# GroupNorm on one core: GpSimd scales 13 channels of a tile instead of 8 and ScalarE three instead of two, so VectorE's share goes from 22 to 16

## The chip, the cores and the metric

The kernel runs on one core of a Trainium2 chip. The metric is device time in microseconds (us). Time before the change: 635.31 us, the median of three runs (635.22 to 635.34). In the profiles PE is TensorE, DVE is VectorE, ACT is ScalarE, POOL is GpSimd and SP is SyncE.

## The reference

`x` is 128 x 1024 x 32 x 16 in bf16, in 32 groups of 32 channels.

```python
def reference(x, g, b):
    G = 32
    ...
    xr = x.reshape(B, G, C // G, H, W)
    mu = xr.mean(axis=(2, 3, 4), keepdims=True)
    var = ((xr - mu) ** 2).mean(axis=(2, 3, 4), keepdims=True)
    xn = (xr - mu) / jnp.sqrt(var + 1e-5)
    xn = xn.reshape(B, C, H, W)
    return xn * g[None, :, None, None] + b[None, :, None, None]
```

## The kernel before

One tile is 128 partitions (4 samples x 32 groups) by 32 channels of 512 numbers: 4 MB. There are 32 tiles. For each tile TensorE sums the channels with 32 matmuls against the unit matrix, VectorE reduces that to the mean, ScalarE sums the squares in two halves, and then the 32 channels are scaled in place, one instruction a channel, because each channel has its own factor and offset. SyncE issues one 4 MB load and one 4 MB store a tile (the first and the last tile's loads and the last two tiles' stores go in four parts). Six tiles fit into memory.

```python
ACT_SHARE = 2
LAST_SHARE = 2      # channels of a tile that ScalarE scales
POOL_SHARE = 8      # channels of a tile that GpSimd scales
...
    def scale_on(key, i, k):
        st = state[i]
        span = st["xt"][:, k * HW : (k + 1) * HW]
        scl = st["scl"][:, k : k + 1]
        bia = st["bia"][:, k : k + 1]
        if key == "act":
            inst = nc.scalar.activation(
                out=span, in_=span, func=ACT.Identity, bias=bia, scale=scl
            )
        else:
            eng = nc.vector if key == "dve" else nc.gpsimd
            inst = eng.tensor_scalar(
                out=span, in0=span, scalar1=scl, scalar2=bia,
                op0=ALU.mult, op1=ALU.add,
            )
        chain(key, inst)
...
    def A(i):
        if not in_parts(i):                 # all tiles but the last two
            for n in range(POOL_SHARE):
                scale_on("pool", i, KC - LAST_SHARE - POOL_SHARE + n)
            for k in range(KC - LAST_SHARE - POOL_SHARE):
                scale_on("dve", i, k)
            ...
    def finish(i):                          # called between the two halves of the next tile's squares
        ...
        for k in range(KC - LAST_SHARE, KC):
            scale_on("act", i, k)
        S(i, 0, NQ)                         # the store
        state.pop(i)
        j = i + AHEAD
        if UPFRONT <= j < NT:
            L(j)                            # the next load, into the buffer of tile i - 1
```

Of the kernel before, what the change touches and what calls it, by code (L numbers as in the profile page):

```python
# [21 lines left out]
QUARTERS = 4  # L22
STORE_IN_PARTS = 2
ACT_SHARE = 2
LAST_SHARE = 2
POOL_SHARE = 8


@with_exitstack
def kernel(  # L30
# [326 lines left out]
# [12 lines that stand above are left out]
                out=span,  # L369
                in0=span,  # L370
                scalar1=scl,
                scalar2=bia,
                op0=ALU.mult,
                op1=ALU.add,
            )
        chain(key, inst)
# [10 lines left out]
    def in_parts(i):  # L387
        return i >= NT - STORE_IN_PARTS

    def A(i):  # L390

        if not in_parts(i):
# [4 lines that stand above are left out]
# [11 lines left out]
    def finish(i):  # L408
        if i < 0 or in_parts(i):
            return  # L410
        for k in range(KC - LAST_SHARE, KC):
            scale_on("act", i, k)
# [47 lines left out]
```

## Time and profile before

| what | before |
|---|---|
| median, us | 635.31 |
| span of the profiled run, us | 633.4 |
| DMA, 130 to 530 us | 431 GB/s, share 1.00 |
| busy: ScalarE, VectorE, PE, GpSimd | 82%, 58%, 46%, 36% |

The costliest groups before (line, engine, operation, names, shapes, count | busy us, mean ns | idle before them and what ended it):

```profile
L244 ACT ACTIVATE ja<-xt,negmean 128x8192 fp8e5<-128x8192 bf16 x60 | 426.7, 7112 | 74.7 <-DVE jd L189 74.7
...
L368 DVE TENSOR_SCALAR xt<-xt,scl,bia 128x512 bf16<-128x512 bf16 x716 | 341.3, 552 | 39.8 <-POOL bia L353 39.8
...
L368 POOL TENSOR_SCALAR xt<-xt,scl,bia 128x512 bf16<-128x512 bf16 x240 | 190.5, 805 | 3.3
...
L363 ACT ACTIVATE xt<-xt,bia,scl 128x512 bf16<-128x512 bf16 x68 | 50.8, 798 | 0.8 <-DVE bia L324 0.8
```

One tile before, from the timeline (start us, length us, engine, what): the scaling on VectorE and GpSimd, the next tile's sum, and SyncE's next load and store.

```profile
320.03 10.76 DVE L368 TENSOR_SCALAR xt<-xt,scl,bia 128x512 bf16<-128x512 bf16 x22 [1.28 <-POOL bia L353]
320.10 6.35 POOL L368 TENSOR_SCALAR xt<-xt,scl,bia 128x512 bf16<-128x512 bf16 x8
...
338.29 0.69 DVE L189 TENSOR_SCALAR_CACHE_REDUCE jd<-pa 128x512 bf16<-128x512 f32 x1 [7.50 <-PE pa L166]
...
338.99 0.34 SPq L101 DMA_DIRECT2D xt<-in_x_dram  x1
...
339.44 0.36 SPq L381 DMA_DIRECT2D out_dram<-xt  x1
```

The scaling is over at 330.8 us, VectorE then idles 7.5 us, and the tile's store leaves at 339.4 us, behind a load. The DMA queue's own list of waits says for what that load had stood (us in total, times, longest us):

```profile
SPq L101 <- DMA out_dram<-xt: 451.3, 26, 19.5
```

The load waits for an earlier store to land, because it goes into that store's buffer. So engine time is spare and DMA time is not. Three stretches before, from the table of stretches (busy us of PE, PEld, DVE, ACT, POOL, then clock, DMA share, GB/s):

```profile
130.00:530.00 400.00, 189.55 (x658) 73.60 (x659) 241.63 (x522) 333.14 (x145) 156.82 (x250) 0.72 1.00 431
...
625.00:630.00 5.00, 0.00 (x0) 0.00 (x0) 0.00 (x0) 0.00 (x0) 0.00 (x0) 0.50 0.25 107
630.00:634.00 4.00, 0.00 (x0) 0.00 (x0) 0.00 (x0) 0.00 (x0) 0.00 (x0) 0.50 0.03 12
```

From 625 us on the DMA is still at work for 8 us, but at a quarter and then a thirtieth of its rate.

### The profile page before, as it was taken

Reading aid. Unit: us, or ns where it says so; the run is one execution under the profiler, and the core shown is the slowest. Engines: PE = TensorE matmul, PEld = TensorE weight load, DVE = VectorE, ACT = ScalarE, POOL = GpSimd, SP = SyncE. Lnnn points to the kernel's source line nnn. Section 1 sums busy time; section 2 is a strip of 40 time slices with the busy share of each in tenths; the row PEclk is TensorE's granted clock in tenths of the full one; section 3 lists DMA queues with packets and bytes.
Section 4 is the critical chain, followed back from the end, with each engine's and each line's share of the span. In section 5 each row is a group of like instructions: output and inputs, shape, how many; then the busy total and the mean of one; then the engine's idle time right before and its main releaser. Section 6 shows DMA issues by size and latency. Waiting matters only on the chain.

```text
span 633.4 us, 3906 instructions
## 1 busy us (share of the span) xinstructions
PE 289.4 (46%) x1025; PEld 113.3 (18%) x1025; DVE 368.9 (58%) x825; ACT 518.1 (82%) x238; POOL 228.4 (36%) x373
## 2 busy tenths in 40 slices
PE   5577604663345633456423655235553355547000
PEld 2223201221112211122101222012221122212000
DVE  0077777767744577545675455754557645567760
ACT  4599999999977798777987788977879778797960
POOL 0044444444442244422444333443324433244100
PEclk9789758766787667876668776687866678668655
DMA  9999999999999999999999999999999999999995
GB/s 367 433 431 419 430 431 430 430 433 430 430 434 433 435 431 429 431 430 428 431 435 426 433 439 439 431 426 433 430 435 430 430 435 430 433 423 439 431 418 228
DMA packets 11062, 268.69 MB, mean 424 GB/s; under 512 B 1312, under 2 KB 1312, under 8 KB 1312
## 3 DMA queue, kind: packets, MB, share of 16 engines
q1 hardware_dynamic: 10944, 268.44, 98.8%
q8 instruction: 8, 0.13, 0.1%
q14 instruction: 14, 0.11, 0.0%
q10 hardware_dynamic: 96, 0.00, 0.0%
HBM read 134.22 MB, written 134.22 MB: 424 GB/s over the span
## 4 chain that ended last, share of the span: by engine, by line
DMA 71%; ACT 10%; PE 9%; DVE 3%; issue 3%; POOL 1%; SPq 0%; DVEq 0%; ACTq 0%; POOLq 0%
DMA out_dram<-xt 41%; DMA xt<-in_x_dram 30%; PE pa L166 9%; ACT ja L244 9%; DVE xt L368 3%; ACT xt L363 1%; SPq L101 0%; POOL scl L337 0%; PE pb L166 0%; POOL shift L343 0%; ACT rstd L308 0%; DVE jd L189 0%; DVE rstd L312 0%; POOL bia L353 0%; DVE jv L292 0%
## 5 line engine op out<-in xcount | busy, mean ns | idle before, releaser
L244 ACT ACTIVATE ja<-xt,negmean 128x8192 fp8e5<-128x8192 bf16 x60 | 426.7, 7112 | 74.7 <-DVE jd L189 74.7
L166 PE MATMUL pa<-xt,eye 128*128 128x512 bf16 x976 | 278.6, 456 | 294.6 <-DMA xt<-in_x_dram 294.6
L368 DVE TENSOR_SCALAR xt<-xt,scl,bia 128x512 bf16<-128x512 bf16 x716 | 341.3, 552 | 39.8 <-POOL bia L353 39.8
L166 PEld LDWEIGHTS <-eye 128*128 128x128 bf16 x1024 | 113.2, 113 | 470.8 <-DMA xt<-in_x_dram 295.9
L368 POOL TENSOR_SCALAR xt<-xt,scl,bia 128x512 bf16<-128x512 bf16 x240 | 190.5, 805 | 3.3
L337 POOL TENSOR_SCALAR scl<-gb,rstd 128x32 f32<-128x32 f32 x31 | 11.1, 358 | 337.0 <-DVE rstd L312 337.0
L189 DVE TENSOR_SCALAR_CACHE_REDUCE jd<-pa 128x512 bf16<-128x512 f32 x32 | 22.0, 688 | 172.3 <-PE pa L166 172.3
L363 ACT ACTIVATE xt<-xt,bia,scl 128x512 bf16<-128x512 bf16 x68 | 50.8, 798 | 0.8 <-DVE bia L324 0.8
L244 ACT ACTIVATE ja<-xt,q 128x4096 fp8e5<-128x4096 bf16 x8 | 29.7, 3708 | 7.0 <-DVE jd L189 6.8
L312 DVE RECIPROCAL rstd<-rstd 128x1 f32<-128x1 f32 x32 | 5.1, 160 | 24.6 <-ACT rstd L308 24.6
L343 POOL TENSOR_SCALAR shift<-scl,negmean 128x32 f32<-128x32 f32 x31 | 11.1, 358 | 3.1
L166 PE MATMUL pb<-xt,eye 128*128 128x512 bf16 x48 | 11.0, 379 | 1.0 <-DMA xt<-in_x_dram 1.0
L244 ACT ACTIVATION_READ_ACCUMULATOR ja<-xt,negmean 128x1 f32 x60 | 11.2, 186 | 0.0
L308 ACT ACTIVATE rstd<-s,v 128x1 f32<-128x1 f32 x30 | 8.8, 295 | 2.8
L353 POOL TENSOR_TENSOR bia<-shift,gb 128x32 f32<-128x32 f32 x31 | 7.8, 251 | 2.6
L216 POOL TENSOR_SCALAR off<-negmean,q 128x1 f32<-128x1 f32 x2 | 0.9, 430 | 20.6 <-DVE jd L189 20.6
L308 ACT ACTIVATE rstd<-var,eps_t 128x1 f32<-128x1 f32 x2 | 0.6, 294 | 7.5 <-DVE jv L292 7.5
L273 POOL TENSOR_SCALAR v<-s 128x1 f32<-128x1 f32 x30 | 5.7, 191 | 2.5
L156 DVE COPY gb<-gb_p 128x64 f32<-128x64 f32 x1 | 0.2, 225 | 5.3 <-PE gb_p L148 5.3
L116 ACT ACT_TABLE_LOAD x1 | 1.3, 1283 | 1.7 <-PEq L444 1.7
L189 DVE DVE_READ_ACCUMULATOR jd<-pa 128x1 f32 x32 | 2.6, 81 | 0.0
L292 DVE TENSOR_SCALAR_CACHE_REDUCE jv<-sq,seed 128x4 f32<-128x4 f32 x2 | 0.4, 216 | 2.9 <-ACT ja L244 2.9
(18 smaller groups left out, 6.1 us busy)
## 6 DMA issues: line engine op xcount, KB each, us to landing
xt<-in_x_dram SPq DMA_DIRECT2D x30, 4096.0 KB, 29.2
out_dram<-xt SPq DMA_DIRECT2D x30, 4096.0 KB, 38.3
xt<-in_x_dram SPq DMA_DIRECT2D x8, 1024.0 KB, 16.4
out_dram<-xt SPq DMA_DIRECT2D x8, 1024.0 KB, 18.8
gb_b<-in_g_dram ACTq DMA_DIRECT2D x1, 2.0 KB, 3.4
gb_b<-in_b_dram ACTq DMA_DIRECT2D x1, 2.0 KB, 5.4
```

The source lines that it names most:

```text
L116: chain("act", nc.scalar.activation(out=warm[:], in_=eps_t[:], func=ACT.Sqrt))
L166: nc.tensor.matmul(out=ps[:], lhsT=eye[:], rhs=st["xt"][:, k * MMN : (k + 1) * MMN], start=(k == lo), stop=(k == hi - 1),),
L189: nc.vector.tensor_scalar(out=jd[:], in0=ps[:], scalar1=-inv_n, scalar2=seed, op0=ALU.mult, op1=ALU.add, accum_out=total[:],),
L244: nc.scalar.activation(out=ja[:, 0:w], in_=st["xt"][:, k * w : (k + 1) * w], func=ACT.Square, bias=bias, scale=scale, accum_out=sq, satura ...
L273: nc.gpsimd.tensor_scalar(out=v0[:], in0=s0[:], scalar1=inv_n, scalar2=EPS, op0=ALU.mult, op1=ALU.add,),
L308: nc.scalar.activation(out=rstd[:], in_=last_sum[:], func=ACT.Sqrt, bias=bias[:], scale=scale),
L312: chain("dve", nc.vector.reciprocal(out=rstd[:], in_=rstd[:]))
L337: nc.gpsimd.tensor_scalar(out=scl[:], in0=gam, scalar1=rstd[:], scalar2=None, op0=ALU.mult),
L343: nc.gpsimd.tensor_scalar(out=shift[:], in0=scl[:], scalar1=st["negmean"][:], scalar2=None, op0=ALU.mult,),
L353: nc.gpsimd.tensor_tensor(out=bia[:], in0=shift[:], in1=bet, op=ALU.add),
L363: inst = nc.scalar.activation(out=span, in_=span, func=ACT.Identity, bias=bia, scale=scl)
L368: inst = eng.tensor_scalar(out=span, in0=span, scalar1=scl, scalar2=bia, op0=ALU.mult, op1=ALU.add,)
```

## The change

The intent is to balance the scaling: VectorE has the most channels, so five of them go to GpSimd and one to ScalarE.

```diff
 ACT_SHARE = 2
-LAST_SHARE = 2
-POOL_SHARE = 8
+LAST_SHARE = 3
+POOL_SHARE = 13
```

## The prediction

> **What bounds the kernel now.** The DMA. The page has the DMA engines at 90% or more in 39 of 40 slices; the table of stretches gives 431 GB/s and a DMA share of 1.00 for 130 to 530 us. The Trainium skill ("DMA: Bandwidth & Descriptors", Specifications) puts the fabric's ceiling at 435 GB/s, and this trace sits there. 268.4 MB at 431 GB/s are 623 us of the 633.4 us span; the rest is the start and the drain of the last stores. A tile (8.39 MB both ways) costs 19.5 us of DMA. The compute engines fit below that: ScalarE 82%, VectorE 58%, GpSimd 36%. On the DMA queue's own list of waits the next load stands 451 us for an earlier store to land. In the timeline VectorE ends its share of a tile at 330.8 us, and that store is issued only at 339.4, behind such a load: 8.6 us of slack.
>
> **What the change does, per tile (30 of 32; the last two don't use GpSimd).**
> - GpSimd 8 -> 13 channels. Eight took 6.35 us, 0.794 each; 13 should take 10.3.
> - VectorE 22 -> 16 channels. The Trainium skill ("SBUF — State Buffer", "SBUF: two separate sides") says VectorE's two-port modes and GpSimd exclude each other through a locked port pair. The trace agrees in effect: beside GpSimd, VectorE starts about 9 channels in 6.5 us (0.72 each), after it 13 in 4.3 us (0.33 each). In 10.3 us of overlap VectorE does about 14, and needs about 0.6 us for the rest: about 11.0 us from first to last, against 10.77 now. Moving six channels off VectorE shortens nothing. VectorE's busy time, stalls included, stays near 341 us (30 x 11.0 + 18 for the last two tiles = 348); GpSimd's rises from 228 to about 350 us.
> - ScalarE 2 -> 3: +0.70 us a tile, so 16.0 -> 16.7 us a tile in the early stretch where it runs without gaps, still under 19.5.
>
> **On the critical path.** In the steady part nothing: 0.2 to 0.5 us more of scaling and 0.7 us more of ScalarE go into slack of 3 us (ScalarE's wait for the sum) and 8.6 us (the store behind the load). In the first 130 us, where ScalarE is back to back, stores come out later by 0.7 us per tile, at most about 5 us; but about two 4 MB transfers (20 us) are queued by then, so the DMA shouldn't run dry. In the tail, tile 29's third ScalarE channel sits in the final chain and delays tile 31 by 0.7 us. About two 1 MB stores are still queued when its first part is ready near 609 us, so most of that is hidden; I count 0 to 0.7 us.
>
> **Prediction.** 635.6 us, 634.5 to 637.5 for 8 in 10. Faster by over 2%: 1%; within 2%: 96%; slower by over 2%: 3%.
>
> **What would show each step.** DMA share 9 in nearly all slices and 431 GB/s in 130 to 530 us; GpSimd's 390 channels near 0.80 us, 10.3 us per tile; VectorE's 16 channels in about 11 us, mean record near 0.7 us instead of 0.55; ScalarE +21 us busy, its wait for the sum 15 to 20 us shorter; the last ScalarE square 0.7 us later.
>
> **What would make it wrong.** If longer GpSimd runs cost VectorE more than one channel's wait each (15 us or more), the next tile's sum, behind it on VectorE, is late and the store's slack used up. If late early stores leave the DMA idle once, the loss (up to 5 us) is never won back. Another DMA order may gain under 1 us.

## More of the kernel before

From the page of the kernel before: busy time of the engines, the DMA engines' busy tenths in 40 slices of the span, and the DMA queues (packets, MB, share of 16 engines' time).

```profile
PE 289.4 (46%) x1025; PEld 113.3 (18%) x1025; DVE 368.9 (58%) x825; ACT 518.1 (82%) x238; POOL 228.4 (36%) x373
...
DMA  9999999999999999999999999999999999999995
...
q1 hardware_dynamic: 10944, 268.44, 98.8%
q8 instruction: 8, 0.13, 0.1%
q14 instruction: 14, 0.11, 0.0%
```

The DMA is busy from end to end and no engine is. Two lines at the bottom are easy to pass over, and I did: besides the 268 MB of data, 22 small transfers of the kind "instruction" ran. They are 0.1% of the DMA's time.

## The result, and the profile after

The changed kernel took 633.87 us (median of 6; 633.60 to 635.21) against 635.26 us (634.84 to 635.89) for the kernel before. The ratio is 0.9982, with a 95% interval of 0.997 to 0.9995. A ratio here is the mean time of one kernel's fast runs over that of the other's in the same rounds, so it is not quite the ratio of the medians. The result is under the predicted range (634.5 to 637.5), on the side of a gain of about 1.1 us, where I had expected a loss of 0 to 0.7 us.

The lines of the page after that answer to those of before:

```profile
PE 293.1 (46%) x1025; PEld 114.4 (18%) x1025; DVE 380.2 (60%) x645; ACT 539.0 (85%) x268; POOL 346.8 (55%) x523
...
DMA  8999999999999999999999999999999999999996
...
q1 hardware_dynamic: 10944, 268.44, 99.0%
q8 instruction: 8, 0.13, 0.1%
q14 instruction: 15, 0.12, 0.0%
```

VectorE has 180 instructions fewer and is busy 11 us longer; ScalarE and GpSimd are busy longer too. Every engine does more time of work, in a shorter span. The groups after:

```profile
L244 ACT ACTIVATE ja<-xt,negmean 128x8192 fp8e5<-128x8192 bf16 x60 | 426.7, 7112 | 52.1 <-DVE jd L189 52.0
...
L368 DVE TENSOR_SCALAR xt<-xt,scl,bia 128x512 bf16<-128x512 bf16 x536 | 352.6, 732 | 40.0 <-POOL bia L353 40.0
L368 POOL TENSOR_SCALAR xt<-xt,scl,bia 128x512 bf16<-128x512 bf16 x390 | 308.7, 806 | 3.4 <-POOL bia L353 0.3
...
L363 ACT ACTIVATE xt<-xt,bia,scl 128x512 bf16<-128x512 bf16 x98 | 72.0, 798 | 0.8 <-DVE bia L324 0.8
```

One tile after, from the timeline:

```profile
319.70 11.06 DVE L368 TENSOR_SCALAR xt<-xt,scl,bia 128x512 bf16<-128x512 bf16 x16 [1.29 <-POOL bia L353]
319.92 10.38 POOL L368 TENSOR_SCALAR xt<-xt,scl,bia 128x512 bf16<-128x512 bf16 x13 [0.26 <-POOL bia L353]
...
337.53 0.69 DVE L189 TENSOR_SCALAR_CACHE_REDUCE jd<-pa 128x512 bf16<-128x512 f32 x1 [6.78 <-PE pa L166]
338.11 0.34 SPq L101 DMA_DIRECT2D xt<-in_x_dram  x1
...
338.56 0.36 SPq L381 DMA_DIRECT2D out_dram<-xt  x1
```

The scaling of a tile is not shorter: sixteen channels on VectorE beside GpSimd take 11.06 us, where 22 took 10.76. As predicted, the two engines hinder each other so much that moving channels saves nothing. The store still leaves some 8 us after the scaling is done. The DMA queue's wait after:

```profile
SPq L101 <- DMA out_dram<-xt: 425.4, 26, 19.0
```

And the stretches after:

```profile
130.00:530.00 400.00, 192.30 (x664) 74.59 (x665) 250.70 (x401) 355.28 (x171) 240.51 (x357) 0.71 1.00 431
...
625.00:630.00 5.00, 0.00 (x0) 0.00 (x0) 0.00 (x0) 0.00 (x0) 0.00 (x0) 0.50 0.31 131
630.00:634.00 4.00, 0.00 (x0) 0.00 (x0) 0.00 (x0) 0.00 (x0) 0.00 (x0) 0.50 0.00 2
```

In the steady part both kernels move 431 GB/s. I added up the bytes in stretches of 5 us over the whole span: from 65 us to 620 us the two kernels stay within 0.45 us of each other's transfers, now one ahead, now the other. So no DMA time was won on the way. What differs is the end: after 625 us the kernel before trickles until 632.4 us, the changed one until 631.0 us.

**Sixteen engines, not one.** The trickle is explained by looking at the 16 DMA engines one by one. The Trainium skill ("DMA: Bandwidth & Descriptors", "Why a DMA increments its semaphore by 16 and not by 1") says that each engine that takes part in a transfer raises the semaphore by one when its own share has landed. The trace agrees: it holds 1248 such landings for 78 transfers, 16 each. So for each transfer one can read when the first and the last of the 16 engines were done. This table is worked out from those records; "lag" is last minus first.

```
last transfer of the run       first engine done   last engine done   lag     span
kernel before                       623.75 us          632.41 us     8.65   633.4
changed kernel                      623.81 us          630.98 us     7.17   631.9
```

The first engine is done at the same time in both. The last one is 8.65 us later before and 7.17 us later after: a difference of 1.48 us, and the spans differ by 1.5 us. Within one trace the lag never shrinks for long. It is 0.6 us in the first transfers, and in the kernel before it climbs from 225 us on in steps that stand between flat stretches:

```
kernel before: lag of the last engine just before and just after a small "instruction" transfer of 8192 B
instruction transfer at   lag before it   next transfers landed at, lag      VectorE instructions started by then
225.4 us                  4.34            231.5: 5.11   241.2: 5.14            318
313.5 us                  5.13            319.5: 5.95   329.2: 5.93            445
402.5 us                  5.94            407.6: 6.91   417.3: 6.89            563
499.1 us                  6.91            505.4: 7.88   515.1: 7.36            696
593.2 us                  7.87            603.3: 8.68   612.9: 8.68            834
```

Each step is 0.77 to 0.97 us. The right column counts VectorE's instructions in the trace: the transfers come 118 to 138 of them apart, and 8192 B in 128 instructions are 64 B each. The reading is that these five are the fetches of VectorE's own instruction stream, each of which holds up one DMA engine, always the same one, by 0.9 us. It is an inference: the trace names neither the owner of such a transfer nor the engine of a landing. That it is always the same engine follows from the lags: at each step the largest of the 16 grows by 0.77 to 0.97 us, while the second largest moves by at most 0.16 us. The DMA share is 1.00, so that engine has no idle time in which to catch up, and between the steps its lag stays; the span ends 1.0 us after the last engine's last landing.

With 718 instead of 897 instructions in VectorE's stream (all rows of the trace; the page counts only the busy ones) there are 6 fetches instead of 7 (by the same counts GpSimd's longer stream has 5 instead of 3, so that the queue's 14 transfers become 15). In the changed kernel the last engine no longer steps at VectorE's fetches (172.4, 284.4, 400.3, 516.2 us); from 225 us to the end it falls back by 3.0 us, before by 4.3 us. The steps are still there, but on an engine that is not the last: at 516.2 us, for example, a lag of 4.64 us becomes 5.58, while the largest stays where it was (5.97 and 5.96). Followed so, VectorE's engine ends 6.3 us after the first, and another one, which creeps, ends last at 7.17. One fetch less is not all of the difference in VectorE's engine: by 280 us its lag was 3.2 us or less here and 5.1 us before, where only one step (0.77 us) had come since 221 us. I did not find where the rest comes from. In the second profile of the changed kernel (e9, below) it ends at 7.5 us, level with the creeping one, and there one step less would account for most of the difference (0.8 to 1.0 of 1.1 us).

Theory A, then: the gain is one fetch of VectorE's stream less on the DMA engine that ends last. Rivals: B, ScalarE's later stores change the order of reads and writes for the better; C, scatter from run to run (the runs of the two kernels overlap); and the plain reading, that work taken off VectorE pays.

### The profile page after: what moved, and what is told of

It reads as the page before. It is cut to its first block, busy times and chain, and to the rows that moved or that the text cites. A ratio compares the mean times of both kernels' runs of the same rounds, so it can differ in the third digit from the quotient of the medians.

```text
span 631.9 us, 3907 instructions
## 1 busy us (share of the span) xinstructions
PE 293.1 (46%) x1025; PEld 114.4 (18%) x1025; DVE 380.2 (60%) x645; ACT 539.0 (85%) x268; POOL 346.8 (55%) x523
## 4 chain that ended last, share of the span: by engine, by line
DMA 67%; ACT 15%; PE 7%; issue 4%; DVE 3%; POOL 0%; SPq 0%; DVEq 0%; ACTq 0%; POOLq 0%
DMA out_dram<-xt 42%; DMA xt<-in_x_dram 25%; ACT ja L244 13%; PE pa L166 7%; DVE xt L368 3%; ACT xt L363 2%; DMA gb_b<-in_g_dram 1%; POOL scl L337 0%; SPq L101 0%; ACT rstd L308 0%; DVE rstd L312 0%; DVE jd L189 0%; POOL shift L343 0%; DVEq L455 0%; DVE bia L324 0%
## 5 line engine op out<-in xcount | busy, mean ns | idle before, releaser
L244 ACT ACTIVATE ja<-xt,negmean 128x8192 fp8e5<-128x8192 bf16 x60 | 426.7, 7112 | 52.1 <-DVE jd L189 52.0
L166 PE MATMUL pa<-xt,eye 128*128 128x512 bf16 x976 | 281.8, 460 | 289.7 <-DMA xt<-in_x_dram 278.5
L368 DVE TENSOR_SCALAR xt<-xt,scl,bia 128x512 bf16<-128x512 bf16 x536 | 352.6, 732 | 40.0 <-POOL bia L353 40.0
L368 POOL TENSOR_SCALAR xt<-xt,scl,bia 128x512 bf16<-128x512 bf16 x390 | 308.7, 806 | 3.4 <-POOL bia L353 0.3
L363 ACT ACTIVATE xt<-xt,bia,scl 128x512 bf16<-128x512 bf16 x98 | 72.0, 798 | 0.8 <-DVE bia L324 0.8
```

Of the source, the lines that this page charges most:

```text
L166: nc.tensor.matmul(out=ps[:], lhsT=eye[:], rhs=st["xt"][:, k * MMN : (k + 1) * MMN], start=(k == lo), stop=(k == hi - 1),),
L244: nc.scalar.activation(out=ja[:, 0:w], in_=st["xt"][:, k * w : (k + 1) * w], func=ACT.Square, bias=bias, scale=scale, accum_out=sq, satura ...
L363: inst = nc.scalar.activation(out=span, in_=span, func=ACT.Identity, bias=bia, scale=scl)
L368: inst = eng.tensor_scalar(out=span, in0=span, scalar1=scl, scalar2=bia, op0=ALU.mult, op1=ALU.add,)
```

## The experiments

### One half of the change at a time

`e1_act3_only` is the kernel before with ScalarE's third channel alone:

```diff
-LAST_SHARE = 2
+LAST_SHARE = 3
```

> ScalarE takes three channels, GpSimd stays at 8, VectorE goes to 21. Theory A (VectorE's instruction fetches): VectorE's stream is about 867 instructions instead of 897, so still 7 fetches of 128 instructions, and the last-finishing DMA engine lags the median by about 8 to 9 us as before: ratio to before 0.999 to 1.001. Rival B (later stores out of a slower ScalarE change the DMA's order for the better): the gain is here in full, ratio about 0.998. Rival C (scatter between executions): ratio within 0.999 to 1.001, no use of instruction counts.

Measured: 635.78 us against 635.60 us, ratio 1.0002 (0.9989 to 1.0014). VectorE's stream has 867 instructions, the lag at the end is 8.81 us. No gain from ScalarE's part, so rival B falls.

`e2_pool13_only` is GpSimd's part alone:

```diff
-POOL_SHARE = 8
+POOL_SHARE = 13
```

> GpSimd takes 13, ScalarE stays at 2, VectorE goes to 17. Theory A: VectorE's stream is about 748 instructions, 6 fetches instead of 7, so most of the gain is here: ratio 0.9975 to 0.999. Rival B: no gain, ratio 0.9995 to 1.001. Rival C: 0.999 to 1.001 by chance.

Measured: 634.46 us against 635.60 us, ratio 0.9985 (0.9972 to 0.9999). The gain is here, in the part that takes five instructions a tile from VectorE. The profile fell on the slowest of the five runs (636.21 us, lag 9.64 us), so its lag says little about the median; it shows how much the lag scatters between executions. VectorE's count alone does not set the lag of one execution: this one has four VectorE fetches after 221 us, where before has five, but stood at 6.84 us already at 350 us (before: 5.93).

### VectorE's instruction count put back, channels left as changed

`e3_after_pad6` is the changed kernel with six tiny instructions a tile on VectorE:

```diff
+    scratch = consts.tile([P, PAD_W], F32)        # PAD_W = 1, PADS = 6
 ...
             for k in range(KC - LAST_SHARE - POOL_SHARE):
                 scale_on("dve", i, k)
+            for _ in range(PADS):
+                chain("dve", nc.vector.memset(scratch[:], 0.0))
```

> The changed kernel with six memsets of one column a tile added on VectorE, so that its instruction count is that of the kernel before (about 898) while its channels stay 16. Theory A: 7 fetches again, the gain is lost: ratio to before 0.9995 to 1.001. Rival B and the plain reading (work moved off VectorE pays): the gain stays, ratio about 0.998, since six memsets are under 0.5 us a tile off the critical path.

Measured: 635.08 us against 635.60 us, ratio 0.9994 (0.9981 to 1.0006); the stream has 868 instructions in the trace (I had expected 898; the trace has 30 semaphore instructions fewer) and the lag is 8.92 us. The gain is gone or nearly so. As the interval still touches that of the changed kernel, both were run once more on one chip.

> The changed kernel once more, on the same chip as the next three. Theory A (VectorE's instruction fetches set the last DMA engine back): ratio to before 0.997 to 0.9995 as in the first measurement. If the first gain was a chance of that chip: 0.9995 to 1.0005.

> The changed kernel with six one-column memsets a tile on VectorE once more, beside the changed kernel itself. Theory A: 1 us above the changed kernel of this call, ratio to before 0.999 to 1.001. If the instruction count does not matter: equal to the changed kernel within 0.3 us.

Measured: the changed kernel 634.02 us (633.90 to 634.41), with the six memsets 634.82 us (634.69 to 635.14), the kernel before 635.12 us. Ratios to before: 0.9981 (0.9968 to 0.9994) and 0.9993 (0.9980 to 1.0005). The two ranges don't overlap: six instructions a tile that do nothing cost 0.8 us. In both padded traces the last engine steps at VectorE's fetches again, five times after 221 us, as in the kernel before: by 0.70 to 0.95 us in e10 and by 0.47 to 0.93 us in e3. The gain of the change repeats, so rival C falls as an explanation of it. The plain reading falls with e3 and e10: the channels are as changed and most of the gain isn't there.

### More of the suspected cost

`e4_before_pad24` is the kernel before with 24 such memsets a tile (the same edit with PADS = 24).

> The kernel before with 24 memsets of one column a tile on VectorE: about 1617 instructions, 12 or 13 fetches instead of 7, each delaying one DMA engine by 0.8 to 1.0 us. Theory A: 4 to 6 us longer, ratio 1.006 to 1.009, the last DMA engine lagging the median by 12 to 15 us. Rival B, C and every theory in which only engine time counts: the memsets are under 2 us a tile and hidden in over 5 us of slack, ratio 0.999 to 1.001.

Measured: 638.95 us against 635.60 us, ratio 1.0051 (1.0037 to 1.0065), lag 12.03 us. That is just under the expected range (1.006 to 1.009): the count of fetches was right, but not all of them fall on the engine while it is the last one. Behind the median engine, in the terms of the expectation, the last one lay 10.3 us and not 12 to 15. The steps of the last engine's lag in this trace, at VectorE's fetches:

```
fetch at   169.6  225.0  273.2  324.8  377.8  424.6  476.4  523.2  579.8 us
lag before   3.90   4.87   5.88   6.69   7.63   8.41   9.38  10.15  11.11
lag after    4.90   5.87   6.69   7.64   8.40   9.39  10.15  11.13  12.11
```

From 160 us on there are nine such fetches, where the kernel before had five, and nine steps of 0.77 to 1.00 us. The first engine was done at 623.97 us, as ever.

But the 24 memsets also take VectorE time, and a control must rule that out. The first one, `e5_before_wide2`, has two wide memsets a tile in their place (2048 bytes wide):

> Control for the 24 memsets (which took 3.0 us of VectorE a tile and cost 0.5%): the kernel before with two wide memsets a tile instead, an estimated 2 to 4.5 us of VectorE time but only 60 more instructions, half a fetch. Theory A (instruction fetches): 7 or 8 fetches, ratio to before 0.999 to 1.002. Rival (the time that the added VectorE work takes is what cost 0.5%): ratio 1.004 to 1.008.

Measured: 635.33 us against 635.01 us, ratio 1.0003 (0.9991 to 1.0016). The control was weak: its memsets took 0.48 us each instead of 1 to 2 us, so it added 1 us of VectorE time a tile and not 3. So it was made again with one long summing instruction a tile, beside the 24 memsets on one chip:

```diff
+            for _ in range(PADS):                 # PADS = 1, PAD_W = 2816, scratch of uint8
+                chain("dve", nc.vector.tensor_scalar(
+                    out=scratch[:], in0=scratch[:], scalar1=1.0, scalar2=None,
+                    op0=ALU.mult, op1=ALU.add, accum_out=scratch_sum[:]))
```

> The kernel before with one long summing instruction a tile on VectorE (2816 bytes wide), an estimated 3 us a tile, as much as the 24 memsets took (2.96 us), in one instruction and its accumulator read: about 957 VectorE instructions, 7 or 8 fetches. Theory A (instruction count): ratio to before 0.999 to 1.002, well below the 24 memsets. Rival (VectorE's time): the same as the 24 memsets, 1.004 to 1.0065.

> The 24 memsets once more on the same chip, 2.96 us of VectorE a tile in 24 instructions: both theories 1.0035 to 1.0065, as measured; the difference to the run before is what counts: theory A 2 to 4 us, the rival none.

Measured against the same runs of the kernel before (634.90 us): the long instruction 634.77 us, ratio 0.9998 (0.9984 to 1.0012); the 24 memsets 638.59 us, ratio 1.0054 (1.0041 to 1.0067). What each adds to VectorE in a tile, from the timelines, first of the long instruction and then of the 24 memsets:

```profile
331.81 3.07 DVE L405 TENSOR_SCALAR_CACHE_REDUCE scratch<-scratch 128x2816 uint8<-128x2816 uint8 x1
```

```profile
332.12 2.97 DVE L401 MEMSET scratch<- 128x1 f32 x24
```

The same time on VectorE, at the same place of the tile; one costs nothing and the other 3.7 us. The pages show what else differs, first the long instruction's, then the memsets':

```profile
span 632.8 us, 3967 instructions
...
q14 instruction: 14, 0.11, 0.0%
```

```profile
span 636.2 us, 4596 instructions
...
q14 instruction: 19, 0.16, 0.1%
```

Five instruction transfers more. So it is the count of VectorE's instructions that costs, not the time they take.

### Less of the suspected cost

`e8_half_dve` gives a wrong result: the kernel before, with VectorE's 22 channels done two at a time with the first one's factor, so in 11 instructions. GpSimd and ScalarE keep their channels.

```diff
-            for k in range(KC - LAST_SHARE - POOL_SHARE):
-                scale_on("dve", i, k)
+            for k in range(0, KC - LAST_SHARE - POOL_SHARE, 2):
+                scale_on("dve", i, k, 2)          # 1024 numbers from channel k on
```

> Wrong result on purpose: the kernel before with VectorE's 22 channels in 11 instructions alone, GpSimd and ScalarE untouched. Theory A: 567 VectorE instructions, 4 fetches instead of 7, its DMA engine no longer last; the steadily drifting one (6.3 to 7.9 us behind the first) decides: ratio 0.9965 to 0.999. Theories without fetches: 0.9995 to 1.0005, since VectorE was not on the critical path.

Measured: 633.55 us against 635.01 us, ratio 0.9975 (0.9962 to 0.9987), 567 instructions in VectorE's stream, lag 7.37 us. As Theory A expected: removing VectorE's instructions, with no channel moved to another engine, gives all of the gain of the change. The count is not all that differs here: VectorE's busy time falls from 369 to 306 us, and the scaling of a tile from 10.76 to 8.68 us. That this time is worth nothing is supported by e13 from the other side only (more time cost nothing). The gain is hardly more than the change's, with 151 instructions fewer than the changed kernel has: other DMA engines lag by 5 to 7 us as well and now end last.

### Does it hold for the other engines' streams?

Here the theory did worse. The transfers of 16384 B on the second instruction queue, eight in all, come every four tiles, which fits TensorE's 64 instructions a tile at 64 B each. `e7_half_pe` (half the matmuls, so half the mean; this still passed the comparison with the reference) and `e6_half_both` (that and VectorE's channels in pairs, a wrong result) halve TensorE's stream:

```diff
-        for k in range(lo, hi):
+        for k in range(lo, hi, 2):
 ...
-                    stop=(k == hi - 1),
+                    stop=(k == hi - 2),
```

> Wrong result on purpose: the kernel before with half the matmuls alone. Theory A: VectorE's DMA engine remains the last, so ratio 0.998 to 1.001; in the profile half as many fetches on the queue that has eight now, and if the steady drift is TensorE's, the second-last engine's drift falls from 0.2 to 0.1 us a tile.

> Wrong result on purpose: the kernel before with half the matmuls (16 a tile) and with VectorE's 22 channels done two at a time in 11 instructions. Theory A, extended to TensorE (a second DMA engine falls behind by about 0.2 us a tile in all traces, some 1 us per fetch of TensorE's stream): VectorE needs about 4 fetches, TensorE 4, so the two engines that lag most fall back to 4 to 6 us behind the first, and the others (5 us in before) decide: 2.5 to 4 us shorter, ratio 0.9935 to 0.997. If the steady drift is not TensorE's fetching, that engine stays 6 to 8 us behind and the ratio is 0.997 to 0.999. Theories without fetches: 0.9995 to 1.0005, the DMA moves the same bytes.

Measured: e7 636.30 us against 635.01 us, ratio 1.0019 (1.0006 to 1.0032), lag 9.82 us; e6 634.31 us, ratio 0.9989 (0.9976 to 1.0003), lag 6.78 us. The queue did have four transfers instead of eight, as expected. But e7 is slower, not equal, and e6 is not the 2.5 to 4 us faster that I expected, and no faster than e8. So fewer fetches of TensorE's stream bring nothing here, and why e7 lost 0.2% I don't know. The drift that e7 was to test, that of the second-last engine, was 0.14 us a tile between 398 and 555 us, where the kernel before had 0.19: less, but not the half that TensorE's fetches alone would give.

`e12_after_poolpad24` puts 24 memsets a tile on GpSimd in the changed kernel (the edit of e3, with the GpSimd engine):

> The changed kernel with 24 one-column memsets a tile on GpSimd: about 1319 GpSimd instructions, 10 fetches instead of 5, an estimated 2 to 3 us of GpSimd time a tile in slack. Theory A, extended to GpSimd (its fetches hold up a DMA engine too): that engine falls back by about 4 to 5 us more and becomes the last, ratio to before 1.000 to 1.005, clearly above the changed kernel. If only VectorE's fetches cost: equal to the changed kernel, 0.997 to 0.9995.

Measured: 635.94 us against 635.12 us for the kernel before and 634.02 us for the changed one, ratio to before 1.0011 (0.9998 to 1.0023), lag 9.58 us. So 24 more instructions a tile on GpSimd cost time too, though less (1.9 us by the medians for about as many extra instructions as in e4). Whether by their count or by their 3.9 us a tile is open, as there was no control with the same time in fewer of them. The way is not the same in the trace: the engine that ends last does not step at fetches but creeps, by about 0.32 us a tile between 350 and 570 us. It is the second last that steps, by about 0.6 us at each of four transfers (375.9, 433.4, 494.4 and 551.9 us) that come 129 GpSimd instructions apart; it ends 2.4 us before the last. An engine that creeps so by about 0.2 us a tile is there in the traces of the kernel before and of the changed one as well; in the changed one it ends last. No record of mine says what makes it creep.

### A version to beat both

`e11_pool16_act3` goes on in the direction of the change: GpSimd 16, ScalarE 3, VectorE 13.

```diff
-POOL_SHARE = 13
+POOL_SHARE = 16
```

> A version that might beat both: GpSimd 16, ScalarE 3, VectorE 13. GpSimd's run grows to an estimated 12.7 us a tile (16 x 0.794), still inside VectorE's wait for the next sum. Theory A: 628 VectorE instructions, 5 fetches instead of 6, but other DMA engines lag 6 to 7 us as well, so at most 0.7 us better than the changed kernel: ratio to before 0.9965 to 0.9985. If the longer scaling reaches the critical path: over 1.000.

Measured: 634.57 us against 635.12 us, ratio 0.9983 (0.9970 to 0.9997), beside 634.02 us and 0.9981 for the changed kernel. No better: VectorE's stream is shorter (628), but the last engine still ends 7.79 us after the first. No version tried beats the changed kernel clearly.

### All in one table

Lag is that of the last of 16 DMA engines behind the first at the last transfer, in the profiled run; the first engine was done between 623.6 and 624.0 us in every one of them.

| run | VectorE instructions | ratio to before | lag, us |
|---|---|---|---|
| before | 897 | 1 | 8.65 |
| changed; again (e9) | 718 | 0.9982; 0.9981 | 7.17; 7.53 |
| e1, ScalarE's part | 867 | 1.0002 | 8.81 |
| e2, GpSimd's part | 747 | 0.9985 | 9.64 (slowest of its runs) |
| e3; e10, count put back | 868 | 0.9994; 0.9993 | 8.92; 8.32 |
| e5, 1 us more of VectorE | 927 | 1.0003 | 8.45 |
| e13, 3 us more of VectorE | 958 | 0.9998 | 8.15 |
| e4; e14, 24 more instructions | 1587 | 1.0051; 1.0054 | 12.03; 11.50 |
| e8, channels in pairs | 567 | 0.9975 | 7.37 |
| e6, pairs and half the matmuls | 567 | 0.9989 | 6.78 |
| e7, half the matmuls | 897 | 1.0019 | 9.82 |
| e11, GpSimd 16 | 628 | 0.9983 | 7.79 |
| e12, 24 more on GpSimd | 718 | 1.0011 | 9.58 |

## Why the prediction was wrong

**Right.** GpSimd's 13 channels take 10.3 us a tile (10.28 to 10.38 measured, 0.806 us each). VectorE's 16 take 11.06 to 11.15 us where I said 11.0, and its record rises from 0.552 to 0.732 us, because the two engines hinder each other; the scaling of a tile got no shorter. ScalarE is 21 us busier. The steady rate stays 431 GB/s. The early stores come later (the fourth at 96.9 instead of 93.1 us), and the bytes moved show no loss from it. The change is small, and within 2%.

**Near.** ScalarE's wait for the sum shrank by 23 us (74.7 to 52.1), not 15 to 20. Its last square was to come 0.7 us later; it ended 0.5 us earlier, at 604.9 instead of 605.4 us, because the last tile's load had come 1.2 us earlier (TensorE starts on it at 574.5 instead of 575.7 us). That load is complete when the slowest engine's share has landed.

**The step that failed** is in the first paragraph: "268.4 MB at 431 GB/s are 623 us of the 633.4 us span; the rest is the start and the drain of the last stores." I took the 16 DMA engines for one engine at 431 GB/s and the 10 us of rest for fixed. It isn't fixed: 8.65 us of it is the lag of one DMA engine behind the first, built up over the whole run, and it depends on how many instructions VectorE's stream has. So "In the steady part nothing" was wrong as well: in the steady part no compute engine's time is on the critical path, but, by the reading above, a fetch of instructions is, for it comes between the data on a DMA engine that is never idle (DMA share 1.00). I had looked at VectorE's instructions as durations alone; the change takes 180 of them away, and e3 and e10 show that most of its gain goes when nearly as many are put back. What I left as a way to be wrong, "another DMA order may gain under 1 us", had neither the cause nor the size.

What the runs put in its place: fetches of VectorE's stream set one DMA engine back by 0.77 to 1.00 us each (traces of before and e4); 690 more instructions, 5.4 fetches, cost 3.4 us (e4) and 3.7 us (e14) by the medians, 0.6 to 0.7 us a fetch; e13 shows that it isn't their time; e3 and e10 take most of the gain away with the channels left as changed; e8 gives it with no channel moved. The change saves 179 instructions in the stream, 1.4 fetches: at 0.6 to 0.9 us, 0.8 to 1.3 us by estimate. Measured: 1.1 us by the ratio and 1.4 us by the medians. That the sizes agree so well is in part luck: in the changed kernel another engine ends last, or level with VectorE's, so the gain is also bounded by that one, as e8 and e11 show.

**Left open.** That the transfers of 8192 B that coincide with the steps are VectorE's is inferred from instruction counts. The record of such a transfer lasts 0.31 us, yet it sets the engine back by 0.9 us; the Trainium skill ("DMA: Bandwidth & Descriptors", "Queues, rings and completion order") says that a DMA engine takes turns between the queues that have work, a packet at a time, which would explain that data has to wait but not how long; no trace here shows the turns. Between 4.2 and 4.4 us of lag are there by 221 us in the traces of before, changed kernel, e8, e13 and e14 alike, with few steps at fetches, and not always on the engine that VectorE's fetches set back later; I did not find its cause. Nor did I find that of the creeping engine, or of e7's loss. One rival was not tested: something other than the fetches that also grows with the number of instructions, such as the records that the trace keeps of them. For VectorE the steps at the fetches speak against it (the nine steps are 8.3 of e4's 12.0 us of lag); for the creeping engine nothing does.

## What to carry to other kernels

In a kernel that is bound by the DMA, ask when each of the DMA engines ends, not only what they do together: the program ends with the slowest of them, and at most 0.1% of foreign traffic that, as the steps suggest, always falls on one engine made half of the tail here (4.3 of 8.65 us). There, the number of instructions has a price of its own, though no engine is short of time: here about 0.6 to 0.9 us for every 128 instructions of VectorE, as long as it is VectorE's fetches that hold up the last DMA engine. Up to there fewer and longer instructions win and padding with cheap ones loses; below the changed kernel's count e8 and e11 gained next to nothing more. And a control for "more instructions" must take the same time in fewer of them, and one must look into the trace whether it did.

## What the Trainium skill lacked or had wrong

- "Runtime: NRT & Kernel Launch", "Instruction fetch mechanics", says that an engine's instructions are refilled in 16 KiB blocks of 256 and that crossing a block costs one bump of the DMA tail, mostly hidden. Here only the transfers that fit TensorE's stream were of 16384 B; those that fit VectorE's and the others on the same queue were of 8192 B, 128 instructions. Whether that is a setting, no run shows. And in a kernel bound by the DMA the fetch is not hidden from the data: each of those that fit VectorE's stream set one DMA engine back by 0.77 to 1.00 us (traces of before from 225 us and of e4 from 169 us).
- "DMA: Bandwidth & Descriptors", Specifications, gives the ceiling of the 16 engines together, 435 GB/s; this case has 431 GB/s in the steady part. No page that I read says that the engines drift apart when all are saturated: 7 to 12 us between the first and the last in these runs, after 0.4 to 0.6 us in the first transfers.
- "SBUF — State Buffer", "SBUF: two separate sides", describes an exclusive lock between GpSimd and VectorE in its two-port modes. The runs agree in effect (VectorE's channel 0.33 us alone, 0.72 us beside GpSimd), and show the consequence for sharing work: 22 + 8 channels took 10.76 us, 16 + 13 took 11.06 us.
